# Sliding and dilated attention into a squared-ReLU layer: row copies, halos and result stores in another order of issue

## The chip, the core and the metric

The kernel runs on one core of a Trainium2 chip. Its time is the device time of one launch in microseconds (us). Before the change, 11 runs gave a median of 309.38 us (307.22 to 313.34). A core has a matrix engine (PE), a vector engine (DVE), a scalar engine (ACT), a general engine (POOL) and a sync engine (SP). Every engine executes its own list of instructions strictly in order and waits on semaphores for the others. In this kernel SP and POOL issue all DMAs: SP the plain copies and the DMA transposes, POOL those that turn fp32 into fp16 on the way. SP and POOL have a DMA queue each.

## What is computed

Eight batch rows of q, k and v, each with 8 heads, 576 positions and 64 elements per head, go through causal attention. Heads 0 to 3 see the last 32 positions ("sliding"), heads 4 to 7 every fourth of the last 128 ("dilated"). The result is a matrix of 4608 tokens by 512 for a feed-forward layer:

```
scores = scale * q @ k.T          # masked: rel in [0,32), or rel in [0,128) and rel % 4 == 0
x = softmax(scores) @ v           # then (row, token) x (head, dim): 4608 x 512
h = x @ w_in                      # 512 x 2048
out = (relu(h) ** 2) @ w_out      # 2048 x 512, fp32
```

## The kernel before

**Two streams on the PE.** The kernel handles attention row by row (`b`, 0 to 7, 576 tokens each) and the feed-forward layer chunk by chunk (`c`, 0 to 8, 512 tokens each). During row `b` it computes chunk `b-1`. The order is written out by hand: `pump(n)` (L512) takes `n` steps of two to four matmuls from the generator of the chunk, and attention calls such `pump`s between its own groups. A chunk is first `ph = w_in @ x` (`mm1_gen`, L312: ReLU into `rt` on ACT, the square into `g` on DVE), then the product with w_out. Chunk 0 does this by rows of w_out (`mm2_by_rows_gen`, L480, four matmuls per output tile and piece of w_out, so that the third piece, `wo[2]`, is first read at the 33rd `po` matmul), chunk 1 plainly (`mm2_gen`, L470), chunks 2 to 8 by a Strassen-like scheme of seven products (`mm2_strassen_gen`, L353) that reads sums of parts of w_out, `wt`. The 8 DVE subtractions that make `wt` (`w_sums`, L334) run between the ReLU steps of chunk 1.

**A row of attention.** `attn_scores` (L692) makes the scores of two sliding and two dilated groups (`ps`, `pz` in PSUM), exponentials on ACT and a mask multiply on DVE into `AT`. It can call hooks after a group: 0 and 1 sliding, 2 and 3 dilated. `attn_values` (rows 1 to 3, L706) and `attn_values_by_dma` (rows 4 to 7, L737) multiply with v (`pav`, `paw`), normalize on DVE (L605, L610) and turn the result into `xT`: on the PE for rows 1 to 3, by DMA transposes on SP (`x_sliding_by_dma`, `x_dilated_by_dma`, then a copy on ACT, `x_from`) for the others. PSUM has two buffers for scores and values (`papool`) and four for the chunk (`pmool`).

**What a row needs first.** From row 2 on, the sliding q and k arrive as `ns` (POOL, cast), are rearranged by one DVE copy into `nr` (`by_token`, L118), stored to DRAM as `dp` (SP, L214) and read back by DMA transposes into `QKTp` (SP, L223). The dilated q and k go from DRAM to DRAM as `dd` (POOL, L204) and by DMA transposes into `QKTd` (SP, L227). v is loaded as fp32 into `sv` and `sd` (SP, L125, L134) and cast by POOL into `vp` and `vd` (L167, L173). A block of queries reads keys of the block before it, so rows of `vp` and `vd` are copied to other partitions, the "halos": on ACT (L182, L188) or by DMA on SP (`halo_sliding_by_dma`, L193; `halo_dilated_by_dma`, L196). `QKTp`, `QKTd`, `vp` and `vd` have two buffers, used by rows in turn; `sv` and `sd` have one.

**What decides the order on SP and POOL.** It is the order of the calls. Before, for rows 4 to 7: after the second sliding value group `copied` makes `nr` and stores `dp`; `first` loads `sv` of the next row after the first dilated transpose; `second` issues the transposes into `QKTp` and `QKTd` and the load of `sd`, and lets POOL cast `sv` once `yd` has landed. Then come the two result halves `ou` and `ov` of the chunk (`leave`, L394), and at the start of the next row the sliding and the dilated halo. `after_transposes` (L234) is a one-element POOL copy out of `QKTd`: POOL waits there for the transposes before it issues `ns` and `dd` of the row after.

Of the kernel before, what the change touches and what calls it, by code (L numbers as in the profile page):

```python
# [13 lines left out]
P = 128  # L14
# [3 lines left out]
def kernel(  # L18
# [9 lines left out]
    nc = tc.nc  # L28

    B, H, S, D = q.shape  # L30
# [196 lines left out]
    def transpose_dilated(b, dd):  # L227
        for i in (1, 0):
            nc.sync.dma_start_transpose(out=QKTd[b % 2][:, i, :, KPAD:], in_=dd[i])


    seen = const.tile([P, 1], FP16, name="seen")

    def after_transposes(b):  # L234
        nc.gpsimd.tensor_copy(seen, QKTd[b % 2][:, 0, 1, KPAD : KPAD + 1])


    nsd = {0: load_qk(0)}
# [49 lines left out]
    for t, w in zip(wi, wi_cols):  # L288
        r = t.rearrange("p d (g f s) -> p d g f s", f=P, s=4)
        wi4 += [r[:, :, g] for g in range(w // 512)]  # L290

    def mm1_half(c, ffc, ph, dmks):
        lo = c * TOKC % XW
        cut = min(TOKC, XW - lo)
        parts = [(0, cut, lo)] + ([(cut, TOKC, 0)] if cut < TOKC else [])
        for dmk in dmks:
            for t0, t1, x0 in parts:
                nc.tensor.matmul(  # L298
                    ph[:, t0:t1],
                    wi4[ffc // 4][:, dmk, :, ffc % 4],  # L300
                    xT[:, dmk, x0 : x0 + t1 - t0],
                    start=(dmk == 0 and t0 == 0),
                    stop=(dmk == NDM - 1),
                    skip_group_check=len(parts) > 1,
                )
# [6 lines left out]
    def mm1_gen(c, g, sums=False, begun=()):  # L312
        for ffc in range(NFF):
            if ffc < len(begun):
                ph = begun[ffc]
            else:
                ph = mm1_begin(c, ffc)
                yield
            mm1_half(c, ffc, ph, (2, 3))
            rt = osb.tile([P, TOKC], FP16, name=f"rt{c}_{ffc}", tag="rt")  # L320
            nc.scalar.activation(rt, ph[:], ACTF.Relu)  # L321
            nc.vector.tensor_mul(g[:, ffc, :], rt, rt)  # L322
            if c == 1 and ffc % 2 == 0:
                next(w_sums)
            if sums and ffc % 4 == 3 and ffc >= HF:
                sum_of_g(g, ffc - 3, ffc + 1)
            yield
# [25 lines left out]
    def mm2_strassen_gen(c, g):  # L353
# [38 lines left out]
            return ot  # L392

        def leave(o, i, js):  # L394
            t0 = c * TOKC + HTOK * i
            m = slice(HM * js[0], HM * (js[-1] + 1))
            nc.sync.dma_start(
                out=out[t0 : t0 + HTOK, m].rearrange("(t p) m -> p t m", p=P), in_=o[:, :, m]
            )

        def add(ot, bank):
            nc.vector.tensor_add(ot, banks[bank], ot)  # L402
# [47 lines left out]
    first_out = []  # L450

    def leave_first():
        t, o = first_out.pop()
        nc.sync.dma_start(
            out=out[t * P : (t + 2) * P, :].rearrange("(t p) m -> p t m", p=P), in_=o
        )

    def store(c, t, po):
        if t % 2 == 0:
            halves[c] = otp.tile([P, 2, DM], FP32, name=f"ot{c}_{t}", tag="ot")  # L460
        ot = halves[c][:, t % 2]
        nc.scalar.copy(ot, po)
        if c:
            nc.sync.dma_start(out=out[(c * 4 + t) * P : (c * 4 + t + 1) * P, :], in_=ot)
        elif t % 2:
            first_out.append((t - 1, halves[c]))
            if t == 1:
                leave_first()

    def mm2_gen(c, g):  # L470
        for t in range(TOKC // P):
            po = pmool.tile([P, DM], FP32, name=f"po{c}_{t}", tag="pm")
            for ffc in range(NFF):
                mm2(c, g, po, t, ffc)
                if ffc % 2 == 1 and ffc < NFF - 1:
                    yield
            store(c, t, po)
            yield
# [213 lines left out]
    def attn_scores(b, gap, less=0, hooks={}):  # L692
        for hp in range(2):
            s_sliding(b, hp)
            if hp in hooks:
                hooks[hp]()
            pump(gap)
        for g in range(2):
            s_dilated(b, g)
            if 2 + g in hooks:  # L700
                hooks[2 + g]()
            if g and b < 3:
                halo_sliding(b, 0)
            pump(gap - less)

    def attn_values(b, gap, wide=False, then=None):  # L706
        xs = x_tiles(b)
        for mp in range(3):
            av_sliding(b, mp, xs)
            if b < 3:  # L710
                if mp < 2:
                    halo_sliding(b, mp + 1)
                else:
                    halo_dilated(b, 0)
            if then and b == 2 and mp == 2:
# [7 lines left out]
        if then and b == 1:  # L723
            then()
# [12 lines left out]
    def attn_values_by_dma(b, then):  # L737
        xs = x_tiles(b)
        for mp in range(3):
            av_sliding(b, mp, xs)  # L740
            if mp == 1:
                then[0]()
            pump(3)
        x_sliding_by_dma(b, xs)
        ys = []
        for t in range(2):
            for a in range(2):
                av_dilated(b, t, a, xs)
                pump(4 + 2 * (a > t))
            ys.append(x_dilated_by_dma(b, t, xs))  # L750
            then[1 + t](ys[t])
        pump(6)
        x_from(b, 0, ys[0])
        pump(7)
        x_from(b, 1, ys[1])
# [79 lines left out]
    leave_first()  # L835
    load_v(2)


# [3 lines left out]
    for b in range(2, 4):  # L842
        pending.append(moe_gen(b - 1))
        nxt = b + 1
        after_transposes(b)
        ns = load_sliding_qk(nxt)
        if b == 2:
            cast_v(b)
        dd = keep_dilated_qk(nxt)
        if b == 3:  # L850
            halo_sliding_by_dma(b)
            halo_dilated_by_dma(b)

        def turn_and_load():
            dp = turn(nxt, ns)
            load_sliding_v(nxt)
            load_dilated_v(nxt, nc.sync)
            transpose_sliding(nxt, dp)
            transpose_dilated(nxt, dd)
            cast_v(nxt)  # L860

        pump(22 if b == 2 else 12)
        attn_scores(b, 4, 0, {3: turn_and_load} if b == 3 else {})
        attn_values(b, b, False, turn_and_load)
        pump(1000)

    for b in range(4, B):
        pending.append(moe_gen(b - 1))
        nxt = b + 1
        if nxt < B:  # L870
# [5 lines left out]
        halo_sliding_by_dma(b)  # L876
        halo_dilated_by_dma(b)
        dps = []

        def copied():  # L880
            if nxt < B:
                dps.append(turn(nxt, ns))

        def first(y):
            if nxt < B:
                load_sliding_v(nxt)

        def second(y):
            if nxt < B:
# [43 lines left out]
```

## Time and profile before

The profile is of one execution, which took 311.5 us itself, 2.1 us more than the median of the 11 runs. Its span, from the first to the last instruction of the program, is 309.6 us; 1.9 us lie around it.

| what | value |
|---|---|
| time of the profiled execution / its span | 311.5 us / 309.6 us |
| busy: PE, DVE, ACT, POOL | 289.0 (93%), 209.6 (68%), 172.9 (56%), 63.2 (20%) us |
| granted PE clock, mean | 0.994 |
| SP's DMA queue: MB, share of the 16 DMA engines | 32.96 MB, 49.6% |
| POOL's DMA queue: the same | 13.63 MB, 25.6% |
| row 1's part of the PE, row 2, row 3 | about 38 to 61.6 us, 61.6 to 94.4, 94.4 to 125.9 |
| row 4, row 5, row 6, row 7 | 125.9 to 155.8 us, to 188.4, to 223.3, to 253.5 |

The boundaries of the rows are the starts of the first `ph` matmuls of the next chunk in the timeline of the PE. After 253.5 us only chunks 7 and 8 are left. Rows 4 and 7 take 29.9 and 30.2 us, rows 5 and 6 take 32.6 and 34.9.

In timelines, a line is: start in us, duration, engine, line of the kernel, operation, output<-inputs, shapes, count, and in brackets the idle time of the engine before it and what ended that. "SPq" is SP's list of DMA issues; the duration there is that of the issue, not of the transfer. In the chain of work that ended last, a DMA's duration runs from its issue to its landing.

### The profile page before, as it was taken

What the parts mean: (1) busy time and instruction counts of PE and PEld (TensorE: products, weight loads), DVE (VectorE), ACT (ScalarE), POOL (GpSimd) and SP (SyncE); (2) the same over time, 40 slices, a digit from 0 to 9 for tenths busy, and PEclk for the clock granted to TensorE, in tenths of its full rate; (3) what the DMA queues carried; (4) which work ended last, traced back from release to release, by engine and by line L of the source; (5) the groups of instructions that cost most, each with busy time, mean ns of one, the idle gap of its engine ahead of it and who ended that gap; (6) DMA issues with size and microseconds to landing.
All of it is one profiled execution on the core that took longest, in us unless ns stands there. A gap on an engine that the chain in (4) does not pass through costs nothing.

```text
span 309.6 us, 6899 instructions
## 1 busy us (share of the span) xinstructions
PE 289.0 (93%) x2762; PEld 193.7 (63%) x2762; DVE 209.6 (68%) x434; ACT 172.9 (56%) x293; POOL 63.2 (20%) x112
## 2 busy tenths in 40 slices
PE   1898998999999999999997999599999999999994
PEld 1554554554555579557886996358855885685584
DVE  7784449668843898499558974779389934834652
ACT  1866638669735942774565545544395436525620
POOL 4471018004405305300234013500230000000000
PEclk9999999999999999999999999989999999999999
DMA  7899997999499999977899689959891131003004
GB/s 114 188 203 214 206 165 135 207 226 219 86 238 194 236 198 174 247 147 138 168 192 260 139 142 199 270 117 142 146 274 30 32 93 61 2 1 136 2 1 137
DMA packets 77616, 47.03 MB, mean 152 GB/s; under 512 B 58480, under 2 KB 69232, under 8 KB 77584
## 3 DMA queue, kind: packets, MB, share of 16 engines
q1 hardware_dynamic: 68832, 32.96, 49.6%
q0 software_dynamic: 8752, 13.63, 25.6%
q8 instruction: 21, 0.34, 0.5%
q14 instruction: 11, 0.09, 0.1%
HBM read 36.70 MB, written 16.52 MB: 172 GB/s over the span
## 4 chain that ended last, share of the span: by engine, by line
PE 78%; DMA 11%; DVE 5%; ACT 2%; issue 1%; SPq 0%; POOL 0%; DVEq 0%; POOLq 0%
PE ph L298 34%; PE pa L375 15%; PE po L441 8%; PE pb L375 7%; DMA vp<-vp 7%; PE pc L375 4%; PE paw L638 3%; DVE AT L564 2%; DMA QKTp<-dp 2%; PE pav L622 2%; DMA ns<-in_q_dram 2%; PE pf L507 2%; PE ps L573 1%; DMA QKTd<-dd 1%; ACT AT L563 1%
## 5 line engine op out<-in xcount | busy, mean ns | idle before, releaser
L298 PE MATMUL ph<-xT,wi 128*128 128x512 f16 (+1 forms) x640 | 135.7, 361 | 0.7 <-ACT xT L675 0.7
L321 ACT ACTIVATE rt<-ph 128x512 f16<-128x512 f32 x144 | 86.2, 608 | 50.7 <-PE ph L298 49.6
L298 PEld LDWEIGHTS <-wi 128*128 128x128 f16 x640 | 68.4, 114 | 46.7 <-issue 2.0
L322 DVE TENSOR_TENSOR g<-rt 128x512 f16<-128x512 f16 x144 | 63.2, 448 | 40.6 <-ACT rt L321 39.3
L375 PEld LDWEIGHTS <-g 128*128 128x128 f16 x448 | 43.3, 98 | 6.1
L375 PEld LDWEIGHTS <-gs 128*128 128x128 f16 x336 | 32.2, 98 | 3.9 <-DVE gs L332 0.3
L441 PE MATMUL po<-wo,g 128*128 128x512 f16 x128 | 33.1, 379 | 0.0
L402 DVE TENSOR_TENSOR ov<-pb,ov 128x512 f32<-128x512 f32 x14 | 9.7, 692 | 31.1 <-PE pb L375 17.4
L375 PE MATMUL pa<-wt,gs 128*128 128x256 f16 x224 | 27.2, 273 | 0.0
L375 PE MATMUL pb<-wt,g 128*128 128x256 f16 x224 | 27.1, 273 | 0.0
L169 POOL CAST vp<-sv 128x512 f16<-128x512 f32 x24 | 14.4, 630 | 54.0 <-DMA sv<-in_v_dram 42.8
L391 ACT COPY ov<-pa 128x512 f32<-128x512 f32 x14 | 8.2, 586 | 30.6 <-PE pa L375 30.6
L177 POOL CAST vd<-sd 128x512 f16<-128x512 f32 (+1 forms) x32 | 22.4, 727 | 11.7 <-DMA sd<-in_v_dram 9.5
L610 DVE TENSOR_TENSOR xd<-paw,rcp_d 80x512 f16<-80x512 f32 (+1 forms) x32 | 21.9, 685 | 1.1
L563 ACT ACTIVATE AT<-pz 128x576 f16<-128x576 f32 x32 | 19.7, 694 | 1.1 <-PE pz L592 0.9
L564 DVE TENSOR_TENSOR AT<-AT,maskp 128x576 f16<-128x576 f16 x32 | 16.4, 526 | 5.7 <-ACT AT L563 4.0
L563 ACT ACTIVATE AT<-ps 128x576 f16<-128x576 f32 x32 | 19.2, 657 | 1.8 <-PE ps L573 1.3
L564 DVE TENSOR_TENSOR AT<-AT,maskd 128x576 f16<-128x576 f16 x32 | 17.6, 578 | 1.7 <-ACT AT L563 0.7
L622 PEld LDWEIGHTS <-AT 128*128 128x128 f16 x192 | 9.5, 99 | 13.4 <-issue 8.3
L391 ACT COPY ou<-pa 128x512 f32<-128x512 f32 x14 | 8.2, 586 | 16.9 <-PE pa L375 15.4
L622 PE MATMUL pav<-vp,AT 128*128 128x65 f16 x192 | 10.9, 196 | 7.1 <-DMA vp<-vp 5.5
L610 DVE TENSOR_TENSOR xs<-pav,rcp_p 96x512 f16<-96x512 f32 x24 | 16.5, 687 | 0.8
(80 smaller groups left out, 277.5 us busy)
## 6 DMA issues: line engine op xcount, KB each, us to landing
sv<-in_v_dram SPq DMA_DIRECT2D x14, 288.0 KB, 5.3
dp<-nr SPq DMA_DIRECT2D x12, 288.0 KB, 3.9
out_dram<-ou SPq DMA_DIRECT2D x6, 512.0 KB, 4.0
out_dram<-ov SPq DMA_DIRECT2D x6, 512.0 KB, 4.4
sd<-in_v_dram SPq DMA_DIRECT2D x8, 320.0 KB, 6.4
ns<-in_k_dram POOLq DMA_DIRECT2D x8, 288.0 KB, 6.7
ns<-in_q_dram POOLq DMA_DIRECT2D x8, 288.0 KB, 7.9
sd<-in_v_dram SPq DMA_DIRECT2D x8, 256.0 KB, 5.6
```

Source lines behind the costliest of these rows:

```text
L169: nc.gpsimd.tensor_copy(vp[b % 2][:, m : m + 2, :, 0:D], sv[:, :, m : m + 2, :].rearrange("p h m d -> p m h d"))
L177: nc.gpsimd.tensor_copy(vd[b % 2][p0:P, t, c : c + 2, :, 0:D], sd[p0:P, t, :, D * c : D * (c + 2)].rearrange("p h (c d) -> p c h d", d=D),)
L298: nc.tensor.matmul(ph[:, t0:t1], wi4[ffc // 4][:, dmk, :, ffc % 4], xT[:, dmk, x0 : x0 + t1 - t0], start=(dmk == 0 and t0 == 0), stop=(dmk ...
L321: nc.scalar.activation(rt, ph[:], ACTF.Relu)
L322: nc.vector.tensor_mul(g[:, ffc, :], rt, rt)
L375: nc.tensor.matmul(banks[bank][:, t], a(k, t), b(k), start=(new and t == 0 and k == 0), stop=(k == HF - 1), skip_group_check=True,)
L391: nc.scalar.copy(ot, banks[A])
L441: nc.tensor.matmul(po, g[:, ffc, t * P : (t + 1) * P], wo[ffc // 4][:, ffc % 4, :], start=(ffc == 0), stop=(ffc == NFF - 1),)
L563: nc.scalar.activation(AT[:, u, 0:UW], ps[:, :, 0 : UW // 2], ACTF.Exp, scale=scale)
L564: nc.vector.tensor_mul(AT[:, u, 0:UW], AT[:, u, 0:UW], mask)
L610: nc.vector.tensor_tensor(out=x, in0=pv, in1=rb, op=ALU.mult)
L622: nc.tensor.matmul(pav[:, i, h * (D + 2) : h * (D + 2) + D + 1], AT[:, 2 * (h // 2) + m // 3, off : off + P], vp[b % 2][:, m, h, 0 : D + 1 ...
```

## The change

- `v` of row 1 (load and sliding cast) comes ahead of the third piece of w_out; the third and fourth piece are issued together after that cast.
- In row 1 the halo `halo_sliding(1, 0)` moves to the second sliding score group. `nr` and `dp` of row 2 are made after the third sliding value group (before: after the first dilated one), and the transposes of row 2 follow at once, `QKTd` first.
- Row 2 starts its scores after 9 steps of the chunk (before 22), row 3 after 8 (before 12). In row 2 a value group is followed by 3 steps (before 2).
- In rows 2 and 3 the next row's `nr` is made after the second sliding value group (before: after the third in row 2, after the last score group in row 3). In rows 4 to 6 it is made after the last score group (before: after the second sliding value group).
- The sliding halo by DMA is issued as soon as `sv` is cast and, in rows 4 to 6, right behind the transposes into `QKTd`; it is ahead of `sd`, and of the results.
- Results of chunk 0, of the second half of chunk 1, and of chunks 2 to 4 are held, and issued behind the next row's `dp`. Chunk 1 is stored in halves of two tiles.
- The eight `w_sums` run in the second product of chunk 1 and no longer in its first.

```diff
-load_w_out((2,))
 load_v(1)
 cast_sliding_v(1)
-load_w_out((3,))
+load_w_out((2, 3))
...
+    def leave_held():
+        while held:
+            held.pop(0)()
...
-            if c == 1 and ffc % 2 == 0:
-                next(w_sums)
...
+                if ffc % 8 == 1:
+                    next(w_sums)
...
-            t0 = c * TOKC + HTOK * i
-            m = slice(HM * js[0], HM * (js[-1] + 1))
-            nc.sync.dma_start(
-                out=out[t0 : t0 + HTOK, m].rearrange("(t p) m -> p t m", p=P), in_=o[:, :, m]
-            )
+            leave_half(c, i, o, slice(HM * js[0], HM * (js[-1] + 1)), 1 < c < 5)
...
-    attn_scores(1, 2, 1)
-    dp = []
-    attn_values(1, 1, True, lambda: dp.append(keep_sliding_qk(2, by_token(2, ns))))
+    attn_scores(1, 2, 1, {1: lambda: halo_sliding(1, 0)})
+    def turn_row_2():
+        dp = keep_sliding_qk(2, by_token(2, ns))
+        transpose_dilated(2, dd)
+        transpose_sliding(2, dp)
+    attn_values(1, 1, True, turn_row_2)
     pump(1000)
-    transpose_sliding(2, dp[0])
-    transpose_dilated(2, dd)
-    leave_first()
     load_v(2)
...
         def turn_and_load():
             dp = turn(nxt, ns)
+            leave_held()
             load_sliding_v(nxt)
-            load_dilated_v(nxt, nc.sync)
             transpose_sliding(nxt, dp)
-            transpose_dilated(nxt, dd)
-            cast_v(nxt)
-        pump(22 if b == 2 else 12)
-        attn_scores(b, 4, 0, {3: turn_and_load} if b == 3 else {})
-        attn_values(b, b, False, turn_and_load)
+            cast_sliding_v(nxt)
+            transpose_dilated(nxt, dd, (1,))
+            halo_sliding_by_dma(nxt)
+            transpose_dilated(nxt, dd, (0,))
+            load_dilated_v(nxt, nc.sync)
+        pump(9 if b == 2 else 8)
+        attn_scores(b, 4)
+        attn_values(b, 3, False, turn_and_load)
...
-        if b > 4:
-            cast_dilated_v(b)
-        halo_sliding_by_dma(b)
+        cast_dilated_v(b)
         halo_dilated_by_dma(b)
         def copied():
             if nxt < B:
-                dps.append(turn(nxt, ns))
-        def first(y):
-                load_sliding_v(nxt)
-        def second(y):
-                transpose_sliding(nxt, dps[0])
-                transpose_dilated(nxt, dd)
-                load_dilated_v(nxt, nc.sync)
-                nc.gpsimd.tensor_copy(seen, y[:, 0, 0, 0:1])
-                cast_sliding_v(nxt)
-        attn_scores(b, 3)
-        attn_values_by_dma(b, (copied, first, second))
+                dp = turn(nxt, ns)
+                leave_held()
+                transpose_sliding(nxt, dp)
+                load_sliding_v(nxt)
+        def loaded(y):
+            if nxt < B:
+                nc.gpsimd.tensor_copy(seen, y[:, 0, 0, 0:1])
+                cast_sliding_v(nxt)
+                transpose_dilated(nxt, dd)
+                halo_sliding_by_dma(nxt)
+                load_dilated_v(nxt, nc.sync)
+        attn_scores(b, 3, 0, {3: copied})
+        attn_values_by_dma(b, loaded)
```

More of the change, by code (lines that the diff above doesn't have):

```diff
@@ L225, in transpose_sliding, with transpose_dilated @@
             nc.sync.dma_start_transpose(out=QKTp[b % 2][:, i, :, PADP:], in_=dp[i])
-    def transpose_dilated(b, dd):
-        for i in (1, 0):
+    def transpose_dilated(b, dd, sides=(1, 0)):
+        for i in sides:
             nc.sync.dma_start_transpose(out=QKTd[b % 2][:, i, :, KPAD:], in_=dd[i])
@@ L234, in after_transposes @@
     def after_transposes(b):
-        nc.gpsimd.tensor_copy(seen, QKTd[b % 2][:, 0, 1, KPAD : KPAD + 1])
+        t = QKTp[b % 2][:, 0, 1, PADP : PADP + 1] if b == 2 else QKTd[b % 2][:, 0, 1, KPAD : KPAD + 1]
+        nc.gpsimd.tensor_copy(seen, t)
     nsd = {0: load_qk(0)}
@@ L290, with leave_half, go @@
         wi4 += [r[:, :, g] for g in range(w // 512)]
+    held = []
+    def leave_half(c, i, o, m, hold):
+        def go():
+            t0 = c * TOKC + HTOK * i
+            nc.sync.dma_start(
+                out=out[t0 : t0 + HTOK, m].rearrange("(t p) m -> p t m", p=P), in_=o[:, :, m]
+            )
+        if hold:
+            held.append(go)
+        else:
+            go()
+    def leave_held():
+        while held:
+            held.pop(0)()
     def mm1_half(c, ffc, ph, dmks):
@@ L449 @@
     halves = {}
[L450 to L456, printed above, removed]
     def store(c, t, po):
@@ L462, in store @@
         nc.scalar.copy(ot, po)
[L463 to L467, printed above, removed]
-                leave_first()
+        if t % 2:
+            leave_half(c, t // 2, halves[c], slice(0, DM), c == 0 or t > 1)
     def mm2_gen(c, g):
@@ L701, in attn_scores @@
                 hooks[2 + g]()
-            if g and b < 3:
+            if g and b == 2:
                 halo_sliding(b, 0)
@@ L714, in attn_values @@
                     halo_dilated(b, 0)
-            if then and b == 2 and mp == 2:
+            if then and mp == (2 if b == 1 else 1):
                 then()
@@ L722, in attn_values @@
         av_dilated(b, 0, 0, xs)
-        if then and b == 1:
-            then()
         pump(gap)
@@ L735, in attn_values, with attn_values_by_dma @@
         x_dilated(b, 1, xs, wide)
-    def attn_values_by_dma(b, then):
+    def attn_values_by_dma(b, loaded):
         xs = x_tiles(b)
@@ L740, in attn_values_by_dma @@
             av_sliding(b, mp, xs)
-            if mp == 1:
-                then[0]()
             pump(3)
@@ L750, in attn_values_by_dma @@
             ys.append(x_dilated_by_dma(b, t, xs))
-            then[1 + t](ys[t])
+        loaded(ys[1])
         pump(6)
@@ L828 @@
         pump(2)
-    attn_scores(1, 2, 1)
-    dp = []
-    attn_values(1, 1, True, lambda: dp.append(keep_sliding_qk(2, by_token(2, ns))))
+    attn_scores(1, 2, 1, {1: lambda: halo_sliding(1, 0)})
[4 more added lines that the diff above has]
+    attn_values(1, 1, True, turn_row_2)
     pump(1000)
-    transpose_sliding(2, dp[0])
-    transpose_dilated(2, dd)
-    leave_first()
     load_v(2)
@@ L855, in turn_and_load @@
             dp = turn(nxt, ns)
+            leave_held()
             load_sliding_v(nxt)
-            load_dilated_v(nxt, nc.sync)
-            transpose_sliding(nxt, dp)
-            transpose_dilated(nxt, dd)
-            cast_v(nxt)
-        pump(22 if b == 2 else 12)
-        attn_scores(b, 4, 0, {3: turn_and_load} if b == 3 else {})
-        attn_values(b, b, False, turn_and_load)
+            transpose_sliding(nxt, dp)
[3 more added lines that the diff above has]
+            transpose_dilated(nxt, dd, (0,))
+            load_dilated_v(nxt, nc.sync)
+        pump(9 if b == 2 else 8)
+        attn_scores(b, 4)
+        attn_values(b, 3, False, turn_and_load)
         pump(1000)
@@ L873 @@
             dd = keep_dilated_qk(nxt)
-        if b > 4:
-            cast_dilated_v(b)
-        halo_sliding_by_dma(b)
+        cast_dilated_v(b)
         halo_dilated_by_dma(b)
-        dps = []
         def copied():
             if nxt < B:
-                dps.append(turn(nxt, ns))
-        def first(y):
-            if nxt < B:
-                load_sliding_v(nxt)
-        def second(y):
-            if nxt < B:
-                transpose_sliding(nxt, dps[0])
-                transpose_dilated(nxt, dd)
-                load_dilated_v(nxt, nc.sync)
+                dp = turn(nxt, ns)
+                leave_held()
+                transpose_sliding(nxt, dp)
+                load_sliding_v(nxt)
+        def loaded(y):
+            if nxt < B:
                 nc.gpsimd.tensor_copy(seen, y[:, 0, 0, 0:1])
                 cast_sliding_v(nxt)
+                transpose_dilated(nxt, dd)
+                halo_sliding_by_dma(nxt)
+                load_dilated_v(nxt, nc.sync)
         pump(3)
-        attn_scores(b, 3)
-        attn_values_by_dma(b, (copied, first, second))
+        attn_scores(b, 3, 0, {3: copied})
+        attn_values_by_dma(b, loaded)
         pump(1000)
```

## The prediction

> **What bounds the kernel now.** The page first: the PE is the bound, and leaves only 20.6 us of the span unused.
>
> ```profile
> span 309.6 us, 6899 instructions
> ...
> PE 289.0 (93%) x2762; PEld 193.7 (63%) x2762; DVE 209.6 (68%) x434; ACT 172.9 (56%) x293; POOL 63.2 (20%) x112
> ```
>
> Then the waits of the PE, to see which idle time could be won. The first load (5.6 and 1.2 us) isn't touched; the rest is below 1 us apart from one line:
>
> ```profile
> PE pt L536 <- DMA ns<-in_k_dram: 5.6, 1, 5.6
> PE pav L622 <- DMA vp<-vp: 5.5, 3, 3.2
> ...
> PE pav L622 <- ACT vp L184: 0.7, 2, 0.5
> ...
> PE ps L573 <- DMA QKTp<-dp: 0.4, 1, 0.4
> ```
>
> The three waits for `vp<-vp`, the sliding halo, stand in the PE's timeline at 167.10 (2.04 us, row 5), 200.37 (3.24, row 6) and 232.22 (0.25, row 7). Row 6:
>
> ```profile
> 196.83 0.29 PE L622 MATMUL pav<-vp,AT 128*128 128x65 f16 x4
> 200.37 0.29 PE L622 MATMUL pav<-vp,AT 128*128 128x65 f16 x4 [3.24 <-DMA vp<-vp]
> 200.49 2.52 PE L298 MATMUL ph<-xT,wi 128*128 128x512 f16 x6
> ```
>
> Six `ph` matmuls take 2.52 us behind the gap; in row 7 they take 1.46. The table of stretches shows why, in its column after the busy time: the granted clock falls to 0.66 once the PE has stood still for 3.24 us.
>
> ```profile
> 200.00:205.00 5.00, 4.63 (x25) 0.66 0.71 143
> 205.00:210.00 5.00, 5.00 (x45) 1.00 0.89 140
> ```
>
> From the second `pav` to the third group takes 4.5 us in row 6 (200.49 to 205.00) and 2.85 in row 7 (232.34 to 235.19): another 1.66 us. Last, SP's timeline, for why the halo is late:
>
> ```profile
> 186.22 3.04 SPq L229 DMA_TRANSPOSE QKTd<-dd  x2
> 189.32 1.35 SPq L137 DMA_DIRECT2D sd<-in_v_dram  x2
> 190.77 0.54 SPq L397 DMA_DIRECT2D out_dram<-ou  x1
> 191.41 0.42 SPq L397 DMA_DIRECT2D out_dram<-ov  x1
> 191.92 1.10 SPq L194 DMA_DIRECT2D vp<-vp  x1
> ```
>
> POOL finished its cast of `vp` at 186.5, but the halo is issued at 191.92, behind 0.58 MB of v and 1 MB of results, and lands at 200.32. It has to wait for the queue, not for its data.
>
> **Rows 5 to 7: what goes away.** The halo comes right behind `QKTd`, whose issue ends at 189.3 in row 6. With only the transposes ahead it should land as in row 3, where it took 2.9 us (101.29 to 104.14): before 193, and the PE asks at 196.8. In row 5 the PE asks 9 us after the start of the row, in row 7 too. So 2.04 + 3.24 + 0.25 + 1.66 go. `QKTp` of row 5, 0.43 us late at 157.68, is issued some 8 us sooner. Together **7.6 us**. No instruction is added or removed but two result issues of chunk 1 (0.4 us each on SP, hidden); all PE work stays.
>
> **Results held** (1 MB a row) leave the place ahead of the halo and stand behind the next `dp`. Behind them on SP are now the transposes into `QKTp`, the load of `sv` and the transposes into `xT`. The first waits for `dp` to land, and so holds the `xT` transposes. Row 5 before: `dp` issued at 171.33, `xT` landed at 177.71, `yd` at 180.54 and 184.50, chunk 5 starts at 188.42. `dp` comes some 5 us sooner (its `nr` at 9.2 us into the row, below), 1 MB more and about 1.2 MB of `QKTp` and `sv` stand ahead: 2.2 MB at the 0.25 to 0.3 MB/us of this queue is 8 us. `xT` then lands near 182 and the first `yd` near 183; the two copies by ACT take 1.3 and 1.1 us and end before 187. I put this at nothing; the cover is some 2 us. There are three result buffers: the second half of chunk 3 takes at 148.1 that of the first half of chunk 2, stored by about 143.
>
> **nr in rows 4 to 6.** It moves ahead of two value groups. It is a DVE copy of 0.75 us that waits for `ns`; behind it in DVE's list are the squares `g` and the first normalization, which frees the PSUM buffer of the third value group. In row 4 DVE ended the last mask at 135.13, 9.2 us into the row, the first normalization at 136.43, and the PE used the buffer at 137.53. With 0.75 us put in, some 0.4 us remain. Is `ns` there? From its first issue to both landings it took 6.8, 7.9, 8.6 and 10.3 us in rows 3 to 6 (102.32 to 109.11 and so on), the long ones beside results and v. In rows 5 and 6 POOL's guard opens at about 0.3 us into the row, since the transposes into `QKTd` follow `yd` at once (before, row 5: 3.9). At 8.6 us `ns` has landed at 8.9 (no wait), at 10.3 at 10.6, and the PE loses 1.0. In row 4 the issue stays near 1.7 and 7.9 gives 9.6: none. The long ones were beside 1 MB of results that no longer stand there, so I take 0.25 us for each of rows 5 and 6, **0.5** in all; ends 0 and 3.
>
> **w_out's third piece.** Its matmul is the 33rd `po`, at 48.07 (two into the group of four at 47.64). Before, it was issued at 23.68 and landed at 42.43. Now it waits for the cast of v, which needs both halves of `sv` (landed at 45.38). With 0.5 MB less on POOL's queue v comes sooner by what one such piece takes there: the second landed 2.8 us after the first, of which v gets about 2.2. So the cast ends near 45.1 and the piece is issued at 45.0. The nearest row is the fourth piece, also behind this cast: issued at 47.18, landed at 52.24, 5.06 us. So it lands at 50.1, and the PE waits **2.0 us**. The Trainium skill ("DMA: Bandwidth & Descriptors", Anatomy of one DMA) gives 2.0 us plus bytes by 436 GB/s, which for 0.52 MB is an estimate of 3.2 us: landing at 48.2, a wait of 0.1. The row decides: same transfer, same place. While the PE waits, ACT and DVE catch up, and the 0.23 + 0.54 + 0.51 us for which it waited on them from 50 to 54 go (the 0.54 also because the halo on ACT moves up). That leaves about 1.4 us at the start of row 2.
>
> **Row 2's early scores.** Nine steps at 0.43 us put them at 65.5 (before 71.15). `ns` of row 2 lands at 56.05 as before, since the bytes on POOL's queue are the same, so `nr` and `dp` are no sooner. Then SP issues `QKTd` (1.31 + 1.51 us, the second after `dd` at 59.0) to 61.4, then `QKTp`, 1.94 us and the second from 63.3. That one took 4.0 us to land (62.73 to 66.74): 67.3. The PE waits 1.8 us for it, or 0.4 if it comes 1.4 late. The two overlap, so I count **1.8** once. Ends: -0.5 (both in time, the 0.54 won) and 3.5.
>
> **Without a price.** `nr` of row 3 comes after `ns` (issued 3 us sooner, behind `QKTp` now). The eight `wt` (0.69 us each) leave a stretch where DVE is 94% busy (70 to 80) for one where it was 66% (80 to 90); a step of 16 matmuls is 3.5 us and takes two, 1.4; uncovered, 0.7 us in one value group. Dilated v comes later: `sd` follows the halo, some 1 us into a row, lands after 5 to 6 us (median 5.6 and 6.4) and is cast by POOL in 3 us, to about 10; the PE needs it at 13.2 (139.08 in row 4), and the dilated halo at 18. SP waits for that cast ahead of the halo, and behind it stands `dp`, ready at about 10 too; were it 2 us late, so would `xT` be, which has that cover. In rows 2 and 3 SP waits for POOL's cast of `sv` between the two `QKTd` transposes, some 10 us ahead of their use. Row 3's scores come 1.7 us sooner; `QKTp` landed at 99.20 before, and is issued some 8 us sooner.
>
> **The sum**, against the profiled execution: 311.5 - 7.6 + 1.8 + 0.5 = 306.2. That one lay 2.1 us above the median of 309.38; part of the halo waits may be its own. From the median it is 304.1. I take the middle, **305.2**.
>
> **Rivals.** *A, all new waits hidden* (chance 0.14): 1.8 + 0.5 go, about 302.9. For it: DMAs have 1 MB less ahead of the transposes of row 2. Against: 65.5 lies before any landing of `QKTp`. *B, the wait moves to `xT`* (0.14): SP stands at `QKTp` until `dp` has landed, results take the bandwidth, and `xT` comes 4 us later than I put it, in rows 4 to 6. Less 2 us of cover that is some 2 us less 0.7 that ACT makes up, a row: 305.2 + 4 = 309. For it: DMA engines are 85 to 100% busy in rows 4 to 6. Against: ACT has 1 to 2 us of idle time ahead of each copy there. *C, DVE stands at nr* (0.16), slower: the rule that each DMA engine serves the queues in turn, packet by packet (the Trainium skill, same page, Queues, rings and completion order), speaks against the change here. `sd` on SP, issued with `ns`, takes turns with it, whatever the order on SP. By the 8.6 us of the row, no wait; if `ns` takes 12, the PE loses 0.3 + 12 - 9.2 - 0.4 = 2.7 us in each of three rows: 305.2 - 0.5 + 8.1 = 312.8. It ends 0.5% slower from about 11.4 us on; the longest seen is 10.3.
>
> The forecast's own case (303.2 to 307.8) has 0.56. About 0.5% is what a measurement of this kernel can tell from no change. Faster by more: 0.56 + 0.14 = 0.70; within: B, 0.14; slower: C, 0.16. The range reaches from below A, with the two ends of -0.5, to B's upper end: 302.0 to 310.5.
>
> **What would show it.** No `pav` wait for `vp<-vp`; the halo landing within 4 us of its issue; clock 1.00 in row 6; rows 5 and 6 at about 30 us, as row 4. A `po` wait for the third piece near 48 us, of 1 to 2 us; a `ps` wait for `QKTp` of 0.4 to 1.8 us near 66. Wrong: `paw`/`pav` waits on DVE behind an `nr` (C), `ph` waits on `xT` at the starts of chunks (B), or a wait for a transpose in rows 2 and 3.

## The result, and the profile after

The changed kernel is slower: its median is 317.30 us (312.55 to 318.75), the kernel before 309.69 us over all runs made on its side, and the ratio of the two is 1.017 (95% interval 1.013 to 1.021). The forecast was 305.2 us and faster. The ratio leaves out runs more than 1.5% above the fastest of their kernel, six of the changed kernel's twelve among them, and so lies below the ratio of the medians, 1.025. The profiled execution of the changed kernel took 315.86 us, 1.4 us less than its median, and that of the kernel before 311.50 us, 1.8 us more than this median of all runs: the two profiles below account for 4.3 of the 7.6 us between the medians. What the other executions have beyond that is not known.

First the page of the changed kernel, to be held against the first fence of the prediction: the PE works 1.2 us more than before (290.2 against 289.0 us), but the span is 4.2 us longer.

```profile
span 313.8 us, 6876 instructions
...
PE 290.2 (92%) x2762; PEld 193.2 (62%) x2762; DVE 209.9 (67%) x434; ACT 172.2 (55%) x293; POOL 63.5 (20%) x112
```

Then what the PE waited for in it:

```profile
PE pa L392 <- ACT ov L408: 5.9, 3, 2.3
...
PE ps L577 <- DMA QKTp<-dp: 1.5, 1, 1.5
...
PE pav L626 <- DVE xs L614: 1.1, 2, 0.7
PE po L454 <- DMA wo<-in_moe_w_out_dram: 0.9, 1, 0.9
```

The line that the change was about, `pav` waiting for `vp<-vp`, is gone. In its place stands one that the page before did not have at all: matmuls of the Strassen product `pa` wait for ACT's copy `ov`, three times, once in each of rows 4 to 6. `ps` for `QKTp`, `pav` for DVE and `po` for the third piece of w_out are the three small waits that the prediction named.

Cutting both timelines of the PE where the chunks begin shows where the 4.2 us come from (us on the PE; a row begins with the chunk computed in it; by these lines row 4 of the kernel before begins at 126.01 and not at 125.9):

| stretch | before | after | what differs in the after |
|---|---|---|---|
| start to row 2 | 61.56 | 63.39 | 2.0 more from the first `ph` on (half clock at 25 us, wait for `wo` 0.89), 0.2 sooner at the start |
| row 2 | 32.81 | 34.19 | wait for `QKTp` 1.51 |
| row 3 | 31.64 | 31.71 | - |
| row 4 | 29.78 | 33.24 | `ov` 2.34, `nr` 0.71 |
| row 5 | 32.63 | 33.79 | halo 2.04 gone, `QKTp` 0.43 gone, `ov` 2.03 and about 1.6 of half clock behind it |
| row 6 | 34.84 | 31.51 | halo 3.24 and its half clock gone, `ov` 1.57 |
| row 7 and rest | 86.3 | 86.0 | halo 0.25 gone |

The wait for `ov` in row 4 can be followed in ACT's timeline of the changed kernel:

```profile
152.37 0.59 ACT L408 COPY ov<-pa 128x512 f32<-128x512 f32 x1 [2.39 <-PE pa L392]
157.25 1.26 ACT L679 COPY xT<-yd 128x640 f16<-128x640 f16 x1 [4.29 <-DMA yd<-xd]
158.41 0.58 ACT L408 COPY ov<-pa 128x512 f32<-128x512 f32 x1
```

and in the PE's:

```profile
155.66 1.04 PE L392 MATMUL pc<-wo,g 128*128 128x256 f16 x8
159.04 1.91 PE L392 MATMUL pa<-wo,gs 128*128 128x256 f16 x16 [2.34 <-ACT ov L408]
```

ACT has nothing to do for 4.29 us: its next instruction is the copy of `yd` into `xT`, and `yd` isn't there. Behind that copy in its list stands the second copy of `ov`, which empties the PSUM buffer `pa`. The Strassen scheme uses that one buffer for the next product, so the PE stands too. `xT` itself is needed only at the next chunk, at 162.53. The reason `yd` is late is in SP's timeline of the changed kernel:

```profile
140.39 1.21 SPq L217 DMA_DIRECT2D dp<-nr  x2
142.11 0.40 SPq L298 DMA_DIRECT2D out_dram<-ou  x1
142.56 1.55 SPq L298 DMA_DIRECT2D out_dram<-ov  x1
144.23 4.70 SPq L225 DMA_TRANSPOSE QKTp<-dp  x2
148.99 1.99 SPq L132 DMA_DIRECT2D sv<-in_v_dram  x2
151.02 3.06 SPq L684 DMA_TRANSPOSE xT<-xs  x2
154.17 2.54 SPq L691 DMA_TRANSPOSE yd<-xd  x2
```

In the kernel before, the same stretch of SP's timeline is:

```profile
138.76 1.13 SPq L217 DMA_DIRECT2D dp<-nr  x2
139.99 3.78 SPq L680 DMA_TRANSPOSE xT<-xs  x2
144.40 1.70 SPq L687 DMA_TRANSPOSE yd<-xd  x1
```

There the first `yd` was issued at 144.40, 18.4 us into row 4 (126.01); now at 154.17, 24.9 us into it (129.29), behind two results, two transposes and two loads. It lands at 157.22.

### The profile page after: what moved, and what is told of

Same layout as the page of the kernel before. It is cut to its first block, busy times and chain, and to the rows that moved or that the text cites. A ratio compares the mean times of both kernels' runs of the same rounds, so it can differ in the third digit from the quotient of the medians.

```text
span 313.8 us, 6876 instructions
## 1 busy us (share of the span) xinstructions
PE 290.2 (92%) x2762; PEld 193.2 (62%) x2762; DVE 209.9 (67%) x434; ACT 172.2 (55%) x293; POOL 63.5 (20%) x112
## 3 DMA queue, kind: packets, MB, share of 16 engines
q1 hardware_dynamic: 68800, 32.96, 50.4%
## 4 chain that ended last, share of the span: by engine, by line
PE 47%; DMA 22%; DVE 16%; issue 4%; POOL 4%; ACT 3%; SPq 3%; POOLq 0%
PE ph L317 21%; PE pa L392 10%; DMA ns<-in_q_dram 6%; PE pb L392 5%; DMA sv<-in_v_dram 5%; PE po L454 5%; DMA wi<-in_moe_w_in_dram 4%; DVE g L341 4%; DVE xd L614 2%; DVE xs L614 2%; PE pc L392 2%; DMA vd<-vd 2%; DMA yd<-xd 2%; DVE gs L348 2%; DVE gs L349 2%
## 5 line engine op out<-in xcount | busy, mean ns | idle before, releaser
L392 PEld LDWEIGHTS <-g 128*128 128x128 f16 x448 | 43.8, 99 | 6.7
L392 PEld LDWEIGHTS <-gs 128*128 128x128 f16 x336 | 32.5, 98 | 10.6 <-issue 6.5
L392 PE MATMUL pb<-wt,g 128*128 128x256 f16 x224 | 28.0, 279 | 0.0
L392 PE MATMUL pa<-wt,gs 128*128 128x256 f16 x224 | 27.2, 273 | 0.0
L177 POOL CAST vd<-sd 128x512 f16<-128x512 f32 (+1 forms) x32 | 23.2, 753 | 8.8 <-DMA sd<-in_v_dram 5.0
L568 DVE TENSOR_TENSOR AT<-AT,maskp 128x576 f16<-128x576 f16 x32 | 18.4, 591 | 6.5 <-ACT AT L567 5.4
L392 PE MATMUL pa<-wo,gs 128*128 128x256 f16 x112 | 14.2, 281 | 5.9 <-ACT ov L408 5.9
L568 DVE TENSOR_TENSOR AT<-AT,maskd 128x576 f16<-128x576 f16 x32 | 16.6, 539 | 2.6 <-ACT AT L567 1.7
L454 PEld LDWEIGHTS <-g 128*128 128x128 f16 x128 | 10.7, 97 | 10.2 <-issue 1.2
```

What stands on the lines that cost most here:

```text
L177: nc.gpsimd.tensor_copy(vd[b % 2][p0:P, t, c : c + 2, :, 0:D], sd[p0:P, t, :, D * c : D * (c + 2)].rearrange("p h (c d) -> p c h d", d=D),)
L392: nc.tensor.matmul(banks[bank][:, t], a(k, t), b(k), start=(new and t == 0 and k == 0), stop=(k == HF - 1), skip_group_check=True,)
L454: nc.tensor.matmul(po, g[:, ffc, t * P : (t + 1) * P], wo[ffc // 4][:, ffc % 4, :], start=(ffc == 0), stop=(ffc == NFF - 1),)
L568: nc.vector.tensor_mul(AT[:, u, 0:UW], AT[:, u, 0:UW], mask)
```

## The experiments

Each is timed against the kernel before on the same chip: x1 to x4 on one, y1 to y4 on a second, z1 to z4 on a third, with medians of 309.43, 309.98 and 309.42 us for the kernel before. "Ratio" is to that kernel, with its 95% interval; across the groups only ratios should be compared. "The first copy of yd" is `x_from(b, 0, ys[0])`.

**x1: the order on SP put back.** In rows 4 to 6, `QKTp` and `sv` stand behind `xT` and `yd` again; all else is as changed.

```diff
-        loaded(ys[1])
+            (first, loaded)[t](ys[t])
...
+        def first(y):
+            if nxt < B:
+                load_sliding_v(nxt)
...
                 dp = turn(nxt, ns)
                 leave_held()
-                transpose_sliding(nxt, dp)
-                load_sliding_v(nxt)
+                dps.append(dp)
...
                 cast_sliding_v(nxt)
+                transpose_sliding(nxt, dps[0])
                 transpose_dilated(nxt, dd)
```

> The changed kernel, with two steps of rows 4 to 6 put back: the transposes into QKTp go behind yd and the load of sv goes between the two yd, as before the change. Theory (ACT stands at yd): in the changed kernel the ACT copy of yd waits for a late DMA, and the result copy ov behind it on ACT holds the PE, 2.3, 2.0 and 1.6 us in rows 4 to 6, plus about 1 us of half clock behind the 2.0. With xT and yd ahead of QKTp and sv, yd lands 4 us or more sooner, all 6.9 us go, the halo still comes in time: ratio to the kernel before about 0.995. Rival (the DMA engines are full, the order only moves the wait): within 2 us of the changed kernel, 1.010 to 1.017.

Measured: 309.48 us, ratio 0.9995 (0.996 to 1.003), span 306.1. The waits for `ov` are gone: the first `yd` lands at 149.81, and ACT copies it without waiting, 23.2 us into row 4, as the theory had it. The results still stand ahead of `xT` and `yd` here, so they alone do not make `yd` too late.

```profile
150.35 0.59 ACT L408 COPY ov<-pa 128x512 f32<-128x512 f32 x1 [2.39 <-PE pa L392]
150.96 1.31 ACT L679 COPY xT<-yd 128x640 f16<-128x640 f16 x1
```

The ratio falls short of the 0.995 expected. With `QKTp` ahead of `QKTd`, POOL issues `ns` 4.3 and 3.6 us into rows 5 and 6, where the changed kernel did it at the rows' start, and `pav` waits for DVE behind `nr`: 0.17, 0.49 and 1.41 us in rows 4 to 6. With 0.43 in row 3, which x2 and x3 have too, that is the line

```profile
PE pav L626 <- DVE xs L614: 2.5, 4, 1.4
```

**x2: the results not held.**

```diff
-            leave_half(c, i, o, slice(HM * js[0], HM * (js[-1] + 1)), 1 < c < 5)
+            leave_half(c, i, o, slice(HM * js[0], HM * (js[-1] + 1)), False)
```

> The changed kernel, with the results of chunks 2 to 4 not held: they are issued behind sd, ahead of the dilated halo and of the next dp. Theory (ACT stands at yd): 1 MB less stands ahead of QKTp, sv, xT and yd, so yd lands 3 to 4 us sooner, the ACT wait of 4.3 us in row 4 falls to 1 or less, and the PE's waits for ov to under 0.5 us each: ratio about 0.998. The price: ns and the dilated halo share the engines with the results, up to 1 us at nr. Rival (engines full): 1.010 to 1.017.

Measured: 312.85 us, ratio 1.011 (1.007 to 1.016), span 311.1. The two waits of the theory shrank (ACT's in row 4 to 0.52 us; the PE waits for `ov` once, 1.05 us, where under 0.5 was expected), but its price was too low: `ns`, now beside the results, makes `nr` late. Its profile has a `pav` wait of 2.17 us in row 4, followed by 3.4 us of half clock, and one of 1.20 in row 6.

```profile
PE pav L626 <- DVE xs L614: 3.8, 3, 2.2
...
PE pa L392 <- ACT ov L408: 1.0, 1, 1.0
```

The ratio is the rival's, and the wait did move in part, from `ov` to `nr`. For the result copies it is a trade: held, they make `yd` late; not held, `nr`.

**x3: ACT's order alone.** No DMA moves. The chunk gets three more steps before the first copy of yd, so that `ov` is copied first.

```diff
-        pump(6)
+        pump(9)
         x_from(b, 0, ys[0])
-        pump(7)
+        pump(4)
         x_from(b, 1, ys[1])
```

> The changed kernel with the first ACT copy of yd three steps of the chunk later, so that it stands behind the second result copy ov on ACT and no longer ahead of it; no DMA is moved. Theory (ACT stands at yd): the PE's waits for ov go, since ov no longer stands behind yd, and the next chunk's xT is still ready: 6 to 7 us less than the changed kernel, ratio about 0.995. Rival (the data are late for the PE in any case): the wait comes back as a wait of ph for xT at the start of the next chunk, 1.5 to 2.3 us a row, ratio 1.010 or more.

Measured: 307.76 us, ratio 0.996 (0.993 to 0.999), span 305.0. Three steps of two or four matmuls turn a kernel 1.7% slower than before into one slightly faster. ACT's timeline in row 4:

```profile
151.13 0.59 ACT L408 COPY ov<-pa 128x512 f32<-128x512 f32 x1 [2.39 <-PE pa L392]
154.62 0.59 ACT L408 COPY ov<-pa 128x512 f32<-128x512 f32 x1 [2.91 <-PE pa L392]
156.10 2.28 ACT L679 COPY xT<-yd 128x640 f16<-128x640 f16 x2 [0.89 <-DMA yd<-xd]
```

`yd` is hardly sooner (landed at 156.08), but the wait for it now stands behind the `ov` that the PE needs, and costs nothing: rows 4 to 6 take 30.10, 30.26 and 29.96 us. So the DMA engines were not short of time for this; the order of two copies on ACT was the price.

**x4: the halo alone.** The kernel before, with the halo of rows 5 to 7 right behind the transposes.

```diff
-        halo_sliding_by_dma(b)
+        if b == 4:
+            halo_sliding_by_dma(b)
...
                 transpose_sliding(nxt, dps[0])
-                transpose_dilated(nxt, dd)
-                load_dilated_v(nxt, nc.sync)
                 nc.gpsimd.tensor_copy(seen, y[:, 0, 0, 0:1])
                 cast_sliding_v(nxt)
+                transpose_dilated(nxt, dd)
+                halo_sliding_by_dma(nxt)
+                load_dilated_v(nxt, nc.sync)
```

> The kernel before, with one step of the change alone: for rows 5 to 7 the sliding halo is issued right behind the transposes into QKTd, ahead of sd and of the results. Theory: the gain of this step is as it was predicted, the halo waits of rows 5 to 7 (5.5 us) and the half clock behind the longest (1.7 us) go and nothing else changes: 7.2 us of the profiled execution, ratio 0.977 to 0.985. Rival (engines full, the wait moves to another transfer): 0.99 to 1.00.

Measured: 307.67 us, ratio 0.997 (0.994 to 0.9995), span 305.1. The halo waits are gone (it is issued at 188.50 in row 6 and lands at 191.04), yet the gain is 1.8 us between medians and 0.3% as a ratio, not 7.2 us. The ratio lies in the rival's range, but its reason doesn't hold: no other transfer took the wait over. What is new in rows 5 and 6 is small, two waits of 0.48 us for a DVE sum:

```profile
PE pa L375 <- DVE gs L332: 1.0, 2, 0.5
```

So the question is what there was to win; y4 answers a part of it.

**y4: the kernel before, profiled once more.**

> The kernel before the change, unaltered, for a second profile. The first one took 311.5 us where the median is 309.4, and the step of the halo alone gained 1.7 us in the median where its profile had promised 7.2. Theory (the profiled execution had unusual halo waits): in a second profile the three halo waits and the half clock come to 2 to 4 us instead of 7.2, since they depend on when the DMA engines serve them. Rival (they are always there, and what is won at the halo is lost elsewhere): 6.5 to 8 us again.

Measured: one execution of 310.11 us, span 308.2. Its halo waits:

```profile
168.14 0.29 PE L622 MATMUL pav<-vp,AT 128*128 128x65 f16 x4 [1.09 <-DMA vp<-vp]
```

```profile
199.90 0.29 PE L622 MATMUL pav<-vp,AT 128*128 128x65 f16 x4 [1.70 <-DMA vp<-vp]
```

```profile
230.81 0.29 PE L622 MATMUL pav<-vp,AT 128*128 128x65 f16 x4 [0.97 <-DMA vp<-vp]
```

3.8 us together, in rows 5 to 7, and no half clock behind them, where the first profile had 5.5 and 1.7: within the 2 to 4 expected. The control z1 below, which has the halo where it was, shows 1.25, 2.63 and 0.72, with half clock behind the second. So these waits vary, and those of the first profile are the longest of the three. That is not the whole of it: rows 5 to 7 take 97.7, 93.8 and 96.2 us in these three profiles and 91.6 in x4's, a gain of 2.2 to 6.1 us where the medians show 1.8. All three executions took longer than the median of their kernel, and x4's took less than its own, so these gains may be large ones; how long the waits are in the median run stays open.

**y1, y2, y3: rows 1 and 2**, all on x3. y1 puts the third piece of w_out ahead of v of row 1 again, y2 paces row 2 as before, y3 does both.

```diff
     nsd[1] = load_qk(1)
+    load_w_out((2,))
...
-    load_w_out((2, 3))
+    load_w_out((3,))
```
```diff
-        pump(9 if b == 2 else 8)
+        pump(22 if b == 2 else 8)
...
-        attn_values(b, 3, False, turn_and_load)
+        attn_values(b, b, False, turn_and_load)
```

> The kernel x3_act_order (changed kernel, first ACT copy of yd later) with w_out's third piece issued ahead of v of row 1 again, as before the change. x3's profile has two new waits in rows 1 and 2: 2.16 us of po for that piece and 1.57 us of ps for QKTp of row 2. Theory (the two overlap, since QKTp comes when it comes): the first goes, and the second grows by about as much as the PE is early, to 2.5 to 3: within 0.7 us of x3, ratio to the kernel before 0.994 to 0.997. Rival (they add): 1.2 us or more less than x3, ratio below 0.992.

> The kernel x3_act_order with row 2 paced as before the change: scores after 22 steps of the chunk (x3: 9), two steps between value groups (x3: 3). Theory: QKTp is there long before, its 1.57 us of waiting go, row 2 takes 32.8 us on the PE as before (x3: 34.25), nothing later depends on the early scores: 1.4 us less than x3, ratio 0.991. Rival (the early start is needed for row 3's transposes and halo): a wait for QKTp or vp in row 3, no gain on x3.

> The kernel x3_act_order with both: w_out's third piece ahead of v of row 1, and row 2 paced as before. Theory: no wait for a DMA is left on the PE after the first load; both waits go (2.16 less what ACT and DVE make up, about 1.2, and 1.57): span about 302.4 us, ratio 0.986 to 0.988. Rival: 0.991 as y2 alone, if v of row 1 comes too late again for its halo on ACT (0.5 us).

Measured: y1 307.56 us, ratio 0.995 (0.993 to 0.998); y2 306.53 us, 0.993 (0.990 to 0.996); y3 307.00 us, 0.992 (0.989 to 0.995).

y1 has the ratio that was expected, but not for the reason given. The wait for the piece is gone from its profile, and the wait for `QKTp` in row 2 did not grow: 1.21 us, where x3 has 1.57. In row 1 DVE makes `paw` wait 0.71 us behind an `nr` that waits for `ns`. Between ratios, what the piece is worth doesn't show.

In y2 row 2 takes 32.81 us on the PE as before, without a wait for `QKTp`. Its ratio is 0.3% below that of x3, and the two intervals overlap. y3 misses the 0.986 to 0.988 expected; its ratio lies within the interval of y2, as its rival had it. Its profiled execution had a half clock at 25 us and waits 0.50 us for `QKTp` in row 3. y2 and y3 have the lowest ratios of this study.

**z1, the control.** ACT's order of x3, in the kernel before.

> Control: the kernel before with nothing but the later first ACT copy of yd, as in x3_act_order. Theory (ACT stands at yd only where SP brings yd late): before the change yd had landed when ACT came to it, so the order of these two copies is worth nothing: ratio 0.997 to 1.003. Rival (the later copy is good in itself, by the 1.3 us that it takes ahead of ov): 0.990 to 0.996.

Measured: 309.28 us, ratio 0.999 (0.996 to 1.002). Where `yd` is in time, the order of the two copies is worth nothing; so x3 gained by the wait and not by the order.

**z2: nr back, on y2.** `nr` of rows 4 to 6 is made after the second sliding value group.

```diff
             av_sliding(b, mp, xs)
+            if mp == 1:
+                copied()
             pump(3)
...
-        attn_scores(b, 3, 0, {3: copied})
+        attn_scores(b, 3)
```

> The kernel y2_row_2_start with nr of rows 4 to 6 after the second sliding value group, as before the change. Theory: nr after the scores made DVE wait for ns only now and then (0.2 to 0.7 us of pav in rows 4 to 6 in the profiles of the changed kernel and its variants); these waits go, but dp comes 3 us later, and with it yd, which is behind the result copy in ACT's order and has 2 us of cover before the next chunk: no difference that can be measured, 0.989 to 0.996. Rival (the earlier nr is needed, now that results, QKTp and sv stand behind dp): ph waits for xT at the chunk starts, 1 to 2 us a row: 1.000 to 1.012.

Measured: 315.47 us, ratio 1.017 (1.013 to 1.022), span 313.6. The rival, beyond its range of 1.000 to 1.012: in row 4 `dp` is issued 13.0 us into the row (y2: 10.3), all behind it on SP is later too, the cover is used up, and the PE waits at the chunks' starts.

```profile
PE ph L317 <- ACT xT L679: 7.5, 6, 2.4
```

So the earlier `nr` pays for the longer queue behind it.

**z3 and z4: the failed step alone.** The kernel before, in whose rows 4 to 6 results, `QKTp` and `sv` follow `dp`, ahead of `xT` and `yd`; z4 adds ACT's order of x3.

```diff
+    held = []
...
+            def go():
+                nc.sync.dma_start(
...
+            if 1 < c < 5:
+                held.append(go)
+            else:
+                go()
...
-                dps.append(turn(nxt, ns))
+                dp = turn(nxt, ns)
+                while held:
+                    held.pop(0)()
+                transpose_sliding(nxt, dp)
+                load_sliding_v(nxt)
...
         def first(y):
-            if nxt < B:
-                load_sliding_v(nxt)
+            pass
...
-                transpose_sliding(nxt, dps[0])
                 transpose_dilated(nxt, dd)
```

> The kernel before with the failed step alone: in rows 4 to 6 the results of chunks 2 to 4 are held and issued behind dp, and QKTp's transposes and the load of sv follow them, ahead of xT and yd. Rows 1 to 3, nr and the issue of the halo stay. Theory: yd comes late as in the changed kernel, and later by up to 3 us since nr is not moved up: the PE waits for ov in three rows, 6 to 12 us with the half clock, while the halo, with no results ahead, wins back 2: ratio 1.013 to 1.032. Rival (the loss needs the other edits, such as the early scores or the nr): 0.995 to 1.005.

> The kernel z3_step_alone with the first ACT copy of yd behind the second ov copy. Theory: most of the waits for ov go; yd is so late without the earlier nr that part of them comes back at the second copy of yd or as ph waiting for xT at the chunk start, up to 2 us a row: ratio 0.992 to 1.010, and at least 1.5 points below z3. Rival: within 0.5 points of z3.

Measured: z3 326.91 us, ratio 1.057 (1.052 to 1.062); z4 315.82 us, 1.022 (1.017 to 1.027). The mechanism is as expected, its size was too small on both. In z3 the waits are 4.79, 5.29 and 4.70 us, and around the end of each the clock is at half for 6.8 us:

```profile
157.61 3.57 PE L377 MATMUL pa<-wo,gs 128*128 128x256 f16 x16 [4.79 <-ACT ov L393]
```

Sixteen matmuls take 3.57 us here and 1.91 at full clock. Rows 4 to 6 take 37.5, 37.9 and 37.3 us. In z4 rows 4 to 6 take 29.8, 34.1 and 32.5 us instead, but chunks 4 to 6 begin with waits of `ph` for `xT`, which also make row 7 34.6 us long (z3: 29.8):

```profile
PE ph L298 <- ACT xT L684: 6.5, 6, 1.8
...
PE ph L298 <- DMA xT<-xs: 1.5, 2, 1.1
```

The difference of the two ratios, 3.5 points, is what ACT's order costs in this kernel.

## Why the prediction was wrong, step by step

**The step that failed** is "Results held": "the two copies by ACT take 1.3 and 1.1 us and end before 187. I put this at nothing; the cover is some 2 us." The transfer came out as sized, in part by luck: the 0.25 to 0.3 MB/us stand in no line that it shows, and the page of the kernel before gives 0.21 for this queue (32.96 MB in 49.6% of 309.6 us). The prediction had the first `yd` of row 5 land near 183, 27.2 us into the row; it landed at 189.35, 26.8 us into it. The use of it was wrong in two ways. It was held against the start of the next chunk, where `xT` is read; what counts is the instruction behind the copy in ACT's list, the second `ov`. And the row used as the measure contained the stall that the change removes: `ov` was copied at 184.25 in row 5 of the profile before, and 183 plus 1.3 for the copy is just in time for that. Take out of the row the 2.04 us of halo wait and the 0.43 for `QKTp`, as the prediction itself did, and `ov` is due at 181.8, so its own sum gives 2.5 us for row 5. Row 5 before, and then after:

```profile
184.25 0.59 ACT L391 COPY ov<-pa 128x512 f32<-128x512 f32 x1 [1.70 <-PE pa L375]
```

```profile
189.37 1.26 ACT L679 COPY xT<-yd 128x640 f16<-128x640 f16 x1 [3.98 <-DMA yd<-xd]
190.54 0.58 ACT L408 COPY ov<-pa 128x512 f32<-128x512 f32 x1
```

Measured in row 5: 2.03, with 2.34 and 1.57 in the rows beside it, and about 1.6 us of half clock (what is left of row 5 when its waits are counted), 7.5 us in all where the prediction put nothing. x3 shows that ACT's order turns the late `yd` into the loss (the same DMAs, `ov` first, the ratio 2.1 points lower), z3 that the step makes it without the other edits, z1 that the order of the copies is harmless without it. Within the step, x1 and x2 show that `QKTp` and `sv` ahead of `yd` are needed for it (x1 keeps the results held and has no such wait), and that the held results add to it (x2 has one wait of 1.05 us).

Rival B put `xT` 4 us later than the prediction and lost some 4 us in all. In the changed kernel `yd` came when predicted, and the place that B named, `ph` waiting for `xT`, has no wait of this kind in rows 4 to 7, there or in x3. It has them where `dp` comes later too and ACT is reordered (z2, z4).

**The halo**: the mechanism was right, and 7.6 us were mis-sized. The waits are gone in every kernel that issues the halo behind `QKTd`. But 7.6 us came from one execution, 2.1 us above the median. Two more profiles with the halo in its old place have 3.8 and 4.6 us of such waits, with no and with one half clock. By itself the step gains 1.8 us between medians (x4). That the halo lands soon was right: 2.9 us from issue to landing (median of rows 4 to 7), where it was 6.1. The prediction saw that its execution was 2.1 us long and took off half of that; it should have asked whether the wait is of a kind that varies.

**The third piece and row 2's scores**: predicted 1.8 us for both, counted once because they overlap. Measured 2.0 from the first `ph` to row 2, and 1.38 in row 2: 1.6 us more. The piece landed at 50.57 (predicted 50.1; 5.1 us from its issue, as the row of before, not the 3.2 estimated from the Trainium skill, "DMA: Bandwidth & Descriptors", Anatomy of one DMA), and `QKTp` of row 2 at 68.82 with 1.51 us of wait. That the two waits overlap isn't borne out: counted from the first `ph`, the PE of y1, which has the piece in time, comes to row 2's scores 1.5 us sooner than that of x3, but `QKTp` lands 1.9 us sooner as well, and the wait stays. What the piece costs varies: the PE waits for it 0.9, 1.1, 0, 2.2, 0.3 and 1.0 us in the six profiles with the piece behind v (the changed kernel, x1, x2, x3, y2, z2).

**nr**: predicted 0.5 us, in rows 5 and 6. In the changed kernel it was 0.71 in row 4: the guard opened 3.3 us into the row (132.57), not 1.7, because `QKTd` of row 4 landed at 131.98. `nr` itself then waits only 0.24 us, so the 0.4 us of cover that the prediction left beside its 0.75 us is not there; in y1's row 4 `nr` doesn't wait at all, and `pav` still waits 0.32. The variants that hold the results have 0 to 1.4 us a row, and together stay inside the range of 0 to 3. Rival C wasn't what happened, but x2 has a wait of its kind, 2.17 us, where `ns` is issued right behind the results. Whether the DMA engines serve the two queues in turn, as C's argument has it, no run here shows.

**Half clock at 25 us**: the profiled execution ran 3.4 us at half clock there, which cost the PE 1.7 us. Up to there both kernels have the same matmuls on the PE, and of the twelve other profiles y3 alone has it, so it is probably chance. The PE's windows of the changed kernel, then of the kernel before (the number behind the count is the granted clock):

```profile
24.00:30.00 6.00, 5.33 (x21) 0.72 1.09 216
```

```profile
24.00:30.00 6.00, 5.30 (x28) 1.00 1.09 215
```

Little of it need be lost in the end. Had the PE come to w_out's third piece 1.7 us sooner, it would have waited some 2.6 us for it instead of 0.89, if the piece had landed at the same time (an estimate from these two numbers). x3, without half clock there, waits 2.16 us and takes 41.73 us from its first `ph` to row 2, the changed kernel 42.15, the kernel before 40.12.

Still open is which part of the 0.7% that y2 gains is due to which of the remaining edits: halo, `wt` and row 3 were not taken apart.

## What to carry to other kernels

When a transfer is moved back, find the instruction that waits for it and ask who stands behind that one on its engine: here a copy that nobody needed for 5 us held the copy that the PE needed at once. Putting the waiter of a late transfer later in the engine's list cost nothing in x3, because what it feeds was needed later still; in z2 and z4, with the transfer later by some 3 us, that cover was gone. And measure slack in a row without the stall that the change removes, in more than one execution where the stall comes from a shared queue.

## What the runs showed of the hardware that was not expected

- Waits of the PE of much the same length were or were not followed by half clock. 3.4 us of it came behind waits of 2.03 us (changed kernel, row 5), 2.17 (x2, row 4), 2.63 (z1, row 6) and 3.24 (first profile), and behind two waits close together in z2 (2.36 and 0.77) and z4 (1.78 and 0.60). None came behind 2.04 (before, row 5), 2.16 (x3, row 1) and 2.34 (changed kernel, row 4). In z3, with waits of 4.7 to 5.3 us, it began before the wait ended and lasted 6.8 us. The table of stretches of the changed kernel has 0.66 (third number from the end) for the 5 us behind the wait of 2.03:

```profile
191.00:196.00 5.00, 4.83 (x30) 3.69 (x30) 1.29 (x2) 1.72 (x3) 2.07 (x5) 0.66 0.91 191
```

- The issue of the same DMAs on SP can take nearly twice as long: the two `QKTp` transposes of row 4 took 2.65 us to issue in the kernel before and 4.70 in the changed one, and all behind them in SP's list is later for that. In rows 4 to 6 the pair took 3.65 to 6.18 us in the eight kernels where two results stand just ahead of it, and 2.65 to 3.06 in the five where none does, x2 among them, which is the changed kernel but for the results. What in the results makes the issue long is not shown.
